# Moving the square root of the softmax shift in an attention backward kernel from ScalarE to a Newton step on VectorE, and spacing the stores of half of q

## The chip, the cores and the metric

One core of one Trainium2 chip. The metric is the device time in microseconds (us) of one execution. Kernels that are compared ran alternately on the same chip. Engine names in the profile: PE is TensorE, PEld its weight loads, DVE is VectorE, ACT is ScalarE, POOL is GpSimd, SP is SyncE, whose queue (SPq) carries transfers. The granted clock is the share of its full speed at which TensorE was allowed to run; "half clock" is 0.5 of it. The semaphore record is the trace's list of the times at which transfers report that they have landed. A pool is a region of on-chip memory from which the kernel takes its tiles.

## The reference

It is the forward pass and all gradients of two blocks on the same tokens: A, a linear attention, and B, a softmax attention with 16 heads of 28 columns that share one k and one v. Only B matters here.

```python
# S = 2048 tokens, D = 448, H = 16 heads, Dh = 28; all bf16
q = (x @ wq).reshape(B, S, H, Dh).transpose(0, 2, 1, 3)
k = x @ wk                              # one k and one v for all heads
v = x @ wv
scores = einsum("bhqd,bkd->bhqk", q, k) * Dh ** -0.5
p = softmax(scores)
o = einsum("bhqk,bkd->bhqd", p, v)
out_b = o.transpose(0, 2, 1, 3).reshape(B, S, H * Dh) @ wo
# ... and the vjp of concatenate([out_a, out_b]) for grad_out
```

The kernel computes exp(score - shift) with a shift for each query and head that is an upper bound of the scores, |q| times the largest |k|. The shift cancels when the row is normalised, so it need not be exact. That square root is what the change moves.

## The kernel before

Three parts follow one another: the linear attention (to about 200 us), a preparation (to 220 us) and the attention core of 512 steps (to 1003 us), with the last gradients behind it. The preparation computes q in four chunks of 512 tokens, writes the shift into spare rows of q, and brings q into token order in DRAM (qn_d), from where the core loads it back (qX).

```python
    def phase_B_pre(pa, cA, awk, psA, io):
        # ... k, v, and the largest |k|^2 per head in kmax2
        for qc in range(NQC):                                  # four chunks of 512 tokens
            # ... q of the chunk: matmuls, ACT copies to qT, DVE squares, row sums in pn
            shift = shifts[qc]
            nc.scalar.activation(out=shift, in_=pn[0:H, :], func=ACT.Sqrt, scale=kmax2[:, 0:1])      # L592
            for g in range(4):
                nc.gpsimd.dma_start(qT[:, g, qs].rearrange(...)[:, 0, :], shift[4 * g:4 * g + 4, :])  # L594
            if qc % 2:                                         # half of q: four transposes, one 1 MB store
                q2 = slice((qc - 1) * 512, (qc + 1) * 512)
                t2 = slice(4 * qc - 4, 4 * qc + 4)
                for g in range(4):
                    nc.sync.dma_start_transpose(qn[:, t2, g * P:(g + 1) * P], qT[:, g, q2])           # L599
                nc.sync.dma_start(qn_d[q2, :].rearrange("(t p) c -> p t c", p=P), qn[:, t2, :])       # L600
    # ... (cut)
    with ExitStack() as pa:                     # buffers of phase A and of the preparation, released together
        # psA ...
        cA = pa.enter_context(tc.tile_pool(name="cA", bufs=1, side="right"))    # holds xa and ga
        cB = pa.enter_context(tc.tile_pool(name="cB", bufs=1, side="right"))    # holds gaB, here the home of qn
        # ...
        phase_B_pre(pa, cA, awk, psA, io)
    # ... the core opens its own pools in the space that is now free: Exp's output eT, its transposes eN, ...
            tc.keep_in_program_order(nc.scalar.activation(out=ex[:], in_=ex[:], func=ACT.Exp))        # dummy Exp
            for u in range(NU + 28):
                # ... scores of step u on PE; a projection of grad_out rides along in some of the first 128 steps
                if hasS:
                    nc.scalar.activation(out=eT(u)[:, 0, :], in_=sp[0][:, :], func=ACT.Exp, scale=scale)   # L904
                # ... (the kernel goes on with the products of step u - 16)
                for a in {10: (0,), 14: (2,), 18: (1,), 22: (3,)}.get(u, ()) or {34: (0,), 42: (2,), 50: (1,), 58: (3,)}.get(u % 64, ()) * (u < 448):
                    # ... qX[qc] quarter a <- qn_d on POOL's queue                                       # L917
                if u == 70:
                    nc.gpsimd.dma_start(wo, ...)
                # ...
                if hasS:
                    # the second Exp of the step (L944), and every fourth step:
                    if u % 4 == 3:
                        nc.sync.dma_start_transpose(ENs[u // 4 % 6][:, :, :], ...)                       # L946
```

## Time and profile before

| | before |
|---|---|
| time, median of the runs beside the changed kernel | 1078.49 us (1077.77 to 1079.88, 4 runs) |
| profiled span, granted PE clock | 1079.1 us, 0.995 |
| first Exp of the core | 220.51 us |
| steps 16, 64, 384, 511 | 241.84, 323.72, 809.95, 1003.18 us |
| from step 511 to the end | 76.0 us |

A step time is the start of the first Exp activation of that step. The granted clock in the 40 slices of the page, in tenths, then the row of Exp in the page's list of the costliest groups (columns: times, mean ns of one, then idle time ahead of it and what ended most of it):

```profile
PEclk9999999998999999999999999999999999999999
...
L904 ACT ACTIVATE eT<-sps 128x512 bf16<-128x512 f32 x512 | 312.6, 611 | 22.9 <-PE dps L653 10.7
```

Exp of the whole core idles 22.9 us, ended most often by a matmul. Second, the reciprocals that this kernel has already, from the groups by form:

```profile
L795 DVE RECIPROCAL rl<-sps 128x4 f32<-128x4 f32 x64 | 10.1, 158 | 0.7 <-ACT eT L904 0.6
L320 DVE RECIPROCAL rden<-rden 128x64 f32<-128x64 f32 x4 | 2.2, 550 | 0.1
```

These two rows are 4 and 64 elements long on every partition. Third, a mark from POOL's timeline that lies before anything that the change touches; it lets one measure the preparation by itself, because the beginning of the program differs by up to 3.9 us between profiled executions (this mark comes at 190.96 in e1 and at 194.90 in e6):

```profile
192.82 0.54 POOL L522 DMA_DIRECT2D wkvT_d<-ga  x1
```

From this mark to the first Exp the kernel before takes 220.51 - 192.82 = 27.69 us.

### The profile page before, as it was taken

Reading aid. Unit: us, or ns where it says so; the run is one execution under the profiler, and the core shown is the slowest. Engines: PE = TensorE matmul, PEld = TensorE weight load, DVE = VectorE, ACT = ScalarE, POOL = GpSimd, SP = SyncE. Lnnn points to the kernel's source line nnn. Section 1 sums busy time; section 2 is a strip of 40 time slices with the busy share of each in tenths; the row PEclk is TensorE's granted clock in tenths of the full one; section 3 lists DMA queues with packets and bytes.
Section 4 is the critical chain, followed back from the end, with each engine's and each line's share of the span. In section 5 each row is a group of like instructions: output and inputs, shape, how many; then the busy total and the mean of one; then the engine's idle time right before and its main releaser. Section 6 shows DMA issues by size and latency. Waiting matters only on the chain.

```text
span 1079.1 us, 40135 instructions
## 1 busy us (share of the span) xinstructions
PE 1027.6 (95%) x16326; PEld 489.1 (45%) x16329; DVE 895.5 (83%) x1792; ACT 876.7 (81%) x1744; POOL 772.1 (72%) x1014
## 2 busy tenths in 40 slices
PE   9999999998999999999999999999999999999998
PEld 5555455443444444444444444444444444444434
DVE  7897400447999999999999999999999999999943
ACT  6463122577999999999999999999999999999622
POOL 6001243327888888888988888988998899888881
PEclk9999999998999999999999999999999999999999
DMA  9979899499999999999999999999999999999973
GB/s 239 165 131 195 161 196 193 88 215 169 202 210 198 179 190 187 197 188 201 183 187 191 201 188 194 204 184 182 193 203 186 193 194 193 196 177 180 221 140 92
DMA packets 669026, 199.36 MB, mean 185 GB/s; under 512 B 646008, under 2 KB 664736, under 8 KB 668840
## 3 DMA queue, kind: packets, MB, share of 16 engines
q1 hardware_dynamic: 656296, 175.23, 95.5%
q0 software_dynamic: 7584, 17.59, 6.9%
q10 hardware_dynamic: 4960, 3.96, 1.4%
q8 instruction: 128, 2.10, 0.8%
q14 instruction: 58, 0.48, 0.2%
HBM read 20.99 MB, written 12.94 MB: 31 GB/s over the span
## 4 chain that ended last, share of the span: by engine, by line
PE 34%; POOL 18%; ACT 18%; DVE 14%; issue 12%; DMA 4%; DVEq 0%; ACTq 0%; POOLq 0%; SPq 0%
POOL dsT L912 13%; PE agen L81 13%; ACT cp L911 9%; ACT eT L944 7%; DVE dsx L975 6%; PE sps L653 5%; PE aacc L81 4%; PE oq L653 4%; DVE dsT L909 3%; DMA eN<-eT 2%; PE dv_acc L653 2%; POOL prod L800 1%; PE dps L653 1%; DMA out_dram<-dsT 1%; DVE R L929 1%
## 5 line engine op out<-in xcount | busy, mean ns | idle before, releaser
L912 POOL TENSOR_TENSOR dsT<-cp,eT 128x512 bf16<-128x512 bf16 x512 | 588.4, 1157 | 104.5 <-ACT cp L911 98.6
L975 DVE STREAM_TRANSPOSE dsx<-dsT 128x512 f32<-128x512 f32 x512 | 357.7, 699 | 2.3 <-DVE R L723 0.2
L653 PEld LDWEIGHTS <-R 128*32 128x32 bf16 (+1 forms) x9184 | 229.5, 94 | 278.8 <-issue 238.7
L909 DVE TENSOR_TENSOR dsT<-dps,eT 128x512 bf16<-128x512 f32 x512 | 341.6, 667 | 16.5 <-PE dps L653 11.7
L904 ACT ACTIVATE eT<-sps 128x512 bf16<-128x512 f32 x512 | 312.6, 611 | 22.9 <-PE dps L653 10.7
L911 ACT ACTIVATE cp<-dps 128x512 bf16<-128x512 f32 x512 | 314.2, 614 | 12.0 <-PE dps L653 10.9
L944 ACT ACTIVATE eT<-sps 128x512 bf16<-128x512 f32 x512 | 320.3, 626 | 0.0
L653 PE MATMUL dk_acc<-dsx,qX 32*32 32x512 bf16 x4096 | 268.3, 376 | 0.0
L653 PE MATMUL dps<-doT,R 32*128 32x256 bf16 x2048 | 248.7, 270 | 1.9 <-ACT cp L911 0.8
L653 PE MATMUL sps<-R,R 32*128 32x256 bf16 (+1 forms) x2240 | 222.1, 274 | 7.6 <-DVE R L879 1.7
L653 PE MATMUL oq<-eT,R 128*32 128x256 bf16 x2048 | 158.3, 275 | 1.4 <-issue 1.4
L653 PE MATMUL oq<-dsT,R 128*32 128x256 bf16 x2048 | 157.1, 275 | 0.1
L653 PEld LDWEIGHTS <-qX 32*32 32x32 bf16 x4096 | 79.8, 89 | 114.4 <-issue 54.1
L653 PE MATMUL dv_acc<-eN,don 128*32 128x512 bf16 x1024 | 98.1, 381 | 3.8 <-DMA eN<-eT 3.8
L81 PEld LDWEIGHTS <-R 128*128 128x128 bf16 (+1 forms) x525 | 41.5, 98 | 41.7 <-issue 12.2
L406 POOL COPY pk<-R 128x256 bf16<-128x256 bf16 x4 | 1.6, 399 | 73.2 <-DVE R L366 73.1
L653 PEld LDWEIGHTS <-don 128*32 128x32 bf16 x1024 | 33.8, 97 | 5.0 <-issue 4.5
L422 DVE TENSOR_TENSOR osb<-aacc,pr 64x448 bf16<-64x448 f32 x2 | 1.2, 616 | 41.1 <-ACT pr L421 24.9
L800 POOL TENSOR_TENSOR prod<-R,oTs 128x128 f32<-128x128 bf16 x64 | 28.0, 438 | 7.7 <-DVE oTs L796 7.4
L929 DVE TENSOR_SCALAR R<-oq 64x256 bf16<-64x256 f32 x64 | 27.3, 427 | 3.6 <-PE oq L653 1.6
L817 PE MATMUL sps<-identB,don 128*32 128x128 bf16 x256 | 18.6, 224 | 12.3 <-POOL don L809 8.4
L81 PE MATMUL agen<-R,R 128*128 128x448 bf16 x128 | 28.6, 352 | 0.0
(232 smaller groups left out, 978.7 us busy)
## 6 DMA issues: line engine op xcount, KB each, us to landing
qX<-qn_d POOLq DMA_DIRECT2D x32, 256.0 KB, 4.3
out_dram<-osb ACTq DMA_DIRECT2D x22, 112.0 KB
qn_d<-gaT SPq DMA_DIRECT2D x2, 1024.0 KB
eN<-eT SPq DMA_TRANSPOSE x128
xa<-in_A_x_dram SPq DMA_DIRECT2D x8, 224.0 KB
ga<-in_grad_out_dram SPq DMA_DIRECT2D x4, 448.0 KB
xa<-in_grad_out_dram POOLq DMA_DIRECT2D x4, 448.0 KB, 12.2
out_dram<-wdq POOLq DMA_DIRECT2D x8, 224.0 KB, 6.3
```

What stands on the lines that cost most here:

```text
L81: nc.tensor.matmul(out_ap, lhsT=lhsT, rhs=rhs, start=start, stop=stop, tile_position=(0, 0))
L406: nc.gpsimd.tensor_copy(out=pk[:, t4, D:512], in_=gqn[:, t4, 3 * P:D])
L653: nc.tensor.matmul(out, lhsT=lhsT, rhs=rhs, start=start, stop=stop, tile_position=pos, skip_group_check=True)
L800: nc.gpsimd.tensor_tensor(out=prod[b][:], in0=dnv, in1=os_, op=ALU.mult)
L817: nc.tensor.transpose(tp2[q:q + 32, qb * P:(qb + 1) * P], don[b][:, qb, h, :], identB[:, :], tile_position=(0, q))
L904: nc.scalar.activation(out=eT(u)[:, 0, :], in_=sp[0][:, :], func=ACT.Exp, scale=scale)
L909: nc.vector.tensor_tensor(out=dst[:, 0, :], in0=dp[0][:, :], in1=ew[:, 0, :], op=ALU.mult)
L911: nc.scalar.activation(out=cp[:, :], in_=dp[1][:, :], func=ACT.Copy)
L912: nc.gpsimd.tensor_tensor(out=dst[:, 1, :], in0=cp[:, :], in1=ew[:, 1, :], op=ALU.mult)
L929: nc.vector.tensor_scalar(out=qT_B[g][64 * hp:64 * hp + 64, qc * 256:(qc + 1) * 256], in0=oq[64:128, 0:256], scalar1=scale, scalar2=None, ...
L944: nc.scalar.activation(out=eT(u)[:, 1, :], in_=sp[1][:, :], func=ACT.Exp, scale=scale)
L975: nc.vector.transpose(out=dsx[b][:, tp, :, :, :].rearrange("p h t c -> p (h t c)").bitcast(F32), in_=dsT[y][:, :, :].rearrange("p h c -> p ...
```

## The change

The intent: ACT loaded the table for Sqrt (at 204.10) and, at the core's entry, the one for Exp (1.28 us at 219.10), while PE waited. The change computes the root on DVE from the bit pattern (a shift gives a first value, one Newton step refines it), does the last of the four roots inside the core, and takes the second half of q off the entry: it is transposed into a buffer of the core and stored in four pieces of 256 KB, steps 34 to 58. It also lets the accumulators of the core rotate in the preparation's PSUM pool.

```diff
-        return xbT, wq_pad, rep, bsel, gaB, ga[:, 8:12, :]
+        return xbT, wq_pad, rep, bsel, xa[:, 0:8, :], ga[:, 8:12, :], [flat(gaB[:, 2 * i:2 * i + 2, :]).bitcast(F32) for i in range(3)]
...
-            shift = shifts[qc]
-            nc.scalar.activation(out=shift, in_=pn[0:H, :], func=ACT.Sqrt, scale=kmax2[:, 0:1])
-            # ... shift rows, and for both halves: four transposes, one store
+            if qc == NQC - 1:
+                break
+            q_shift(pn, shifts[qc], qs, tmp)
+            if qc == 1:
+                for g in range(4):
+                    nc.sync.dma_start_transpose(qn[:, :, g * P:(g + 1) * P], qT[:, g, 0:1024])
+                nc.sync.dma_start(qn_d[0:1024, :].rearrange("(t p) c -> p t c", p=P), qn)
...
+    def q_shift(pn, shift, qs, tmp):
+        a, y, r = (t[0:H, :] for t in tmp)
+        nc.scalar.activation(out=a, in_=pn[0:H, :], func=ACT.Identity, bias=eps[:, 0:1], scale=kmax2[:, 0:1])
+        nc.vector.tensor_scalar(out=y.bitcast(mybir.dt.int32), in0=a.bitcast(mybir.dt.int32), scalar1=1, scalar2=None,
+                                op0=ALU.logical_shift_right)
+        nc.vector.tensor_scalar(out=y, in0=y, scalar1=0.485 * 2.0 ** 63.5, scalar2=None, op0=ALU.mult)
+        nc.vector.reciprocal(out=r, in_=y)
+        nc.vector.tensor_tensor(out=r, in0=r, in1=a, op=ALU.mult)
+        nc.vector.scalar_tensor_tensor(out=shift, in0=r, scalar=0.25, in1=y, op0=ALU.mult, op1=ALU.add)
+        # ... the four small writes of the shift, as before
...
-        psA = psc.enter_context(tc.tile_pool(name="psAcc", bufs=1, space=bass.MemoryType.PSUM))
+        # psA of the preparation stays open; SB, DB, oq, dk_acc are taken from it, dv_acc at u == 1
...
-            tc.keep_in_program_order(nc.scalar.activation(out=ex[:], in_=ex[:], func=ACT.Exp))
+            qn = pqb_.tile([P, 8, 512], BF16, name="qX")
+            for g in range(4):
+                nc.sync.dma_start_transpose(qn[:, :, g * P:(g + 1) * P], R1[:, g, 1024:2048])
...
+                if u == 1:
+                    q_shift(*last_shift, [...])                # the last chunk, after the first Exp of step 1
+                    dv_acc = psA.tile([P, 512], F32, name="aacc")
...
+                for n in {34: (0,), 42: (1,), 50: (2,), 58: (3,)}.get(u, ()):
+                    nc.gpsimd.dma_start(qn_d[1024 + 256 * n:1280 + 256 * n, :].rearrange("(t p) c -> p t c", p=P),
+                                        qn[:, 2 * n:2 * n + 2, :])
-                for a in {10: (0,), 14: (2,), 18: (1,), 22: (3,)}.get(u, ()) or {34: (0,), ...}.get(u % 64, ()) * (u < 448):
+                for a in {10: (0,), 14: (2,), 18: (1,), 22: (3,), 66: (0,), 70: (2,), 74: (1,), 78: (3,)}.get(u, ()) or {
+                        34: (0,), 42: (2,), 50: (1,), 58: (3,)}.get(u % 64, ()) * (96 < u < 448):
-                if u == 70:
+                if u == 86:
```

## The prediction

> **What bounds the kernel now.** I read the page first, then the busy time by stretch, then the timeline of the stretch that the change touches, then the chain of waits and the matmul timeline there.
>
> ```profile
> PE 1027.6 (95%) x16326; PEld 489.1 (45%) x16329; DVE 895.5 (83%) x1792; ACT 876.7 (81%) x1744; POOL 772.1 (72%) x1014
> ...
> PE   9999999998999999999999999999999999999998
> DVE  7897400447999999999999999999999999999943
> ACT  6463122577999999999999999999999999999622
> ```
>
> From slice 10 on every engine is near full: that is the attention core, 512 steps u, each with two Exp activations of 128x512. In front of it lie the linear-attention part and a short preparation (slices 7 and 8). The change touches the preparation's end and the core's first 80 steps only. By stretch (columns: us, busy time of PE, PEld, DVE, ACT, POOL, then the granted clock, DMA share, GB/s):
>
> ```profile
> 218.00:226.00 8.00, 5.84 (x46) 2.56 (x45) 2.22 (x5) 6.17 (x11) 2.85 (x7) 0.79 0.87 203
> ...
> 250.00:270.00 20.00, 16.88 (x274) 7.29 (x275) 14.61 (x29) 14.57 (x29) 13.27 (x16) 0.84 1.20 185
> ...
> 400.00:1000.00 600.00, 576.23 (x11316) 267.20 (x11304) 584.90 (x1136) 593.07 (x1188) 529.75 (x630) 1.00 1.13 191
> ```
>
> In the steady core ACT is busy 593 of 600 us, so any start-up delay of ACT that is not made up moves the end one for one. Only the first and second rows show slack and a reduced clock. The entry itself:
>
> ```profile
> 212.47 5.94 SPq L599 DMA_TRANSPOSE gaT<-R  x4
> ...
> 218.41 0.68 ACT L592 ACTIVATE R<-aacc,kmax 16x512 bf16<-16x512 f32 x1 [0.93 <-PE aacc L81]
> ...
> 219.10 1.28 ACT L883 ACT_TABLE_LOAD   x1
> 219.28 0.49 PE L653 MATMUL sps<-R,R 32*128 32x256 bf16 x5 [0.79 <-DVE R L605]
> ...
> 220.51 0.58 ACT L904 ACTIVATE eT<-sps 128x512 bf16<-128x512 f32 x1
> ...
> 220.64 0.36 SPq L600 DMA_DIRECT2D qn_d<-gaT  x1
> 221.14 0.37 PE L653 MATMUL sps<-R,R 32*128 32x256 bf16 x3 [1.37 <-ACT eT L904]
> ```
>
> The last Sqrt (L592) ends at 219.09, the table for Exp is loaded, and the first Exp of the core starts at 220.51. It starts BEFORE the store of the first half of q (L600, issued 220.64): in this kernel Exp does not wait for that store. Remember this. Later in the entry the matmuls wait twice for transposes of Exp's output:
>
> ```profile
> 249.97 1.04 PE L653 MATMUL dv_acc<-eN,don 128*32 128x512 bf16 x6 [1.35 <-DMA eN<-eT]
> ...
> 265.91 0.61 PE L653 MATMUL dv_acc<-eN,don 128*32 128x512 bf16 x6 [2.41 <-DMA eN<-eT]
> ```
>
> They are late because one queue carries, one after the other, q's eight transposes, two 1 MB stores and then these. Counting the L904 activations gives the step times: u=0 at 220.51, u=16 at 241.84, u=64 at 323.72, u=128 at 422.89; the steady pace is about 1.52 us, and 1.545 where projections still ride along. So 48 steps from u=16 should take 74.2 us and take 81.9: 7.7 us are lost there.
>
> **What the skill says.** "ScalarE: Activation LUTs", section What ACT_TABLE_LOAD costs: about 1283 ns each, plus a drain; the trace has 1.28 us. Section Table sets: copy and identity stand in every set, so Identity needs no switch; the built program of after has one table load where before has three, which agrees. "TensorE: Matmul & The Clock Gate", section The HAM clock gate: after idling, the array runs at half clock for a window of about 3.4 us. The 0.79 above is one such window in 8 us: (8 - 3.41/2)/8 = 0.79; and 250 to 270 at 0.84 fits two. "DMA: Bandwidth & Descriptors", section Issuing engines are not separate DMA queues: moving stores to another issuing engine relieves no DMA engine, only the order. The DMA share, above 1.1 in the steady core, agrees.
>
> **The change part by part.**
> (1) Removed: the Sqrt, two table loads of 1.28 us and the dummy Exp (0.20). Only the second load lies at the entry: 218.41 to 220.51 could shrink to a start near 218.7, at most 1.8 us, and PE's idle 0.79 and 1.37 us would go with it, also because the score banks now rotate in the pool of the preparation.
> (2) Added: per chunk, one Identity (0.67 as Sqrt had) and five VectorE operations on 16x512 f32. By the rows for similar work (reduce of 16x512: 672 ns; reciprocal of 128x64: 550; f32 sum of 64x448: 616) I take 0.6 us each: 3 us a chunk, four times. VectorE has room (3.4 busy of 8 us from 210 to 218), so this is latency. But the built program of after puts the Identity of chunk 1 BEHIND the four q copies of chunk 2, and two squares of the next chunk between its five operations. Before, that activation starts at 209.82. After: the fourth copy ends about 212.9, Identity 213.6, the chain about 217.2. From 210.48 (end of the activation) to the first transpose at 212.47 took 2.0 us, so the transposes of the first half start near 219.3 instead of 212.5.
> (3) Moved: the first half of q in token order now lies in the first 8 KB of xa, not in gaT. xa's space is reused by Exp's output tiles. The wait list of the first Exp in the built after-program names the store of that half; in before its list ends at older transfers. So the first Exp must wait: transposes start 219.3, plus 8.15 (before: 212.47 to landing of the fourth at 220.62 by the semaphore record) = 227.4; store 5.2 (220.64 to 225.80 in the same record) = 232.6. First Exp at 232.5 instead of 220.5: **+12.0**. The gain of (1) is buried beneath it.
> (4) The first 16 steps took 21.3 us with one half-clock window. After a 12 us stop PE certainly starts cold, for one to two windows (each costs up to 1.7 us), and the last chunk's five VectorE operations (3 us) sit in front of the projection copies at u=1: **+1.9**.
> (5) The second 1 MB store leaves the queue in front of the second Exp transpose, and with Exp 12 us late the queue has drained. Both waits at u=20 and u=28 go: step 21 took 3.78 us and step 29 4.19, steps 30 and 31 2.25 and 1.83 at half clock, against 1.5 to 1.6: 2.2 + 2.6 + 0.7 = **-5.5**. A further stop of 1.4 us at u=49 (PE, "issue", while a q load is in flight) may or may not recur: **-0.5**.
> (6) Four stores of 256 KB on POOL's queue at u=34 to 58, four loads of q moved to u=66 to 78: about 4 x 0.6 us more on POOL and denser loads: **+0.5**.
> Sum: 1078.1 + 12.0 + 1.9 - 5.5 - 0.5 + 0.5 = 1086.5. I take 1085, as the first half's transposes and store are now less disturbed and may be quicker.
>
> **The rivals.**
> R1, the intent: Exp follows the last copies at once, no table load, no half clock, store out of the way. It would give -1.8, -1.7, -5.5: 1069 to 1071. For it: the listed waits are real and are the only visible DMA waits. Against it: the wait list in (3). It holds only if the store lands by 219, which needs transposes before about 206, when chunk 1 is not computed yet.
> R2, the wait exists but the store is not the bound: transposes unhindered take 6 us and the store 4: Exp at 229.5, +9; with all of (5) regained, 1081 to 1083.
> R3, the late start leads to a new queue behind it: q's second four transposes, the last shift's small writes (which wait for them on POOL) and q loads at u=10 to 22 now meet the Exp transposes; the waits at u=20 and 28 stay. Then nothing is regained: 1091 to 1093.
> R4, VectorE's chain delays the squares and PE in the preparation: at most 1 to 2 us, and hidden beneath the 12.
>
> **Range and chances.** 1082 (R2) to 1087 is the body; R3 is the upper tail, a partly right R1 the lower. 1078 to 1092 should hold it 8 times in 10. 2% is 21.6 us: faster would need under 1056.5, more than the whole loss of the entry (about 12); slower over 1099.6, twice my delay. So 0.01, 0.97, 0.02.
>
> **What would show it.** The timeline of ACT: first Exp near 232, its wait ended by the DMA qn_d<-xa; if it starts at 219, step (3) is wrong and R1 holds. SP's timeline: first transpose of q near 219, store near 227. The clock: a half-speed window right at the first Exp. PE's waits for eN<-eT: gone (5), or still there (R3). u=16 near 255.7, u=64 near 332. Two table loads less, none near the entry. The steady pace from 400 to 1000 must not move; if it does, the prediction is wrong in kind.

## The result

The changed kernel is correct and takes 1103.89 us (1101.12 to 1105.31, 4 runs) against 1078.49. The ratio is 1.0231, 95% interval 1.0207 to 1.0255: slower. A ratio is the mean time of one kernel's runs over that of the other's runs of the same rounds, so not quite the ratio of the medians. Executions over 1.5% slower than the fastest of the same kernel are left out of the means. The profiled run of the changed kernel is its fastest (1101.12), span 1099.4 us, clock 0.983, and that of the kernel before (1080.88) is slower than its four timed runs, so the profiles differ by 20.3 us where the medians differ by 25.4. For the other 5 us no trace was kept.

The page of the changed kernel, the rows that answer to those of before (busy time by engine, the clock by slice, the row of Exp), and then two groups by form:

```profile
PE 1032.9 (94%) x16329; PEld 490.5 (45%) x16329; DVE 915.8 (83%) x1812; ACT 874.9 (80%) x1741; POOL 773.8 (70%) x1018
...
PEclk9999999959899999999999999999999999999999
...
L913 ACT ACTIVATE eT<-aacc 128x512 bf16<-128x512 f32 x512 | 312.9, 611 | 44.5 <-DMA qn_d<-xa 14.8 <-PE aacc L660 11.3 <-PE agen L660 11.2
```

```profile
L612 DVE RECIPROCAL gaT<-gaT 16x512 f32<-16x512 f32 x3 | 10.0, 3335 | 0.0
L613 DVE TENSOR_TENSOR gaT<-gaT 16x512 f32<-16x512 f32 x3 | 2.0, 666 | 0.0
```

Exp's idle time has doubled from 22.9 to 44.5 us, and 14.8 us of it is one wait for a transfer. The clock has one slice at half speed (5 in the ninth slice). DVE has 20.3 us more work, of which four reciprocals are 13.3: each takes 3.33 us, not 0.6. The entry, from the timeline:

```profile
191.12 0.53 POOL L523 DMA_DIRECT2D wkvT_d<-ga  x1
...
219.97 3.33 DVE L612 RECIPROCAL gaT<-gaT 16x512 f32<-16x512 f32 x1
220.35 5.56 SPq L596 DMA_TRANSPOSE xa<-R  x4
...
227.85 0.36 SPq L597 DMA_DIRECT2D qn_d<-xa  x1
228.37 7.02 SPq L892 DMA_TRANSPOSE qX<-R  x4
232.78 0.60 ACT L913 ACTIVATE eT<-aacc 128x512 bf16<-128x512 f32 x1 [14.75 <-DMA qn_d<-xa]
233.43 0.58 PE L660 MATMUL aacc<-R,R 32*128 32x256 bf16 x3 [13.89 <-ACT eT L913]
...
236.09 3.34 DVE L612 RECIPROCAL dsT<-dsT 16x512 f32<-16x512 f32 x1
...
241.25 1.01 PE L82 MATMUL agen<-R,R 128*128 128x256 bf16 x4 [3.26 <-DVE R L886]
...
242.83 0.60 ACT L913 ACTIVATE eT<-aacc 128x512 bf16<-128x512 f32 x1 [3.73 <-PE aacc L660]
```

Read from the top: the mark comes at 191.12, so this execution is 1.70 us ahead of the one before when the preparation starts. The transposes of the first half start at 220.35 (before: 212.47), the store at 227.85, and the first Exp at 232.78, right behind the landing of that store, which the semaphore record of the trace puts at 232.22. From the mark to the first Exp it is 41.66 us against 27.69, so 13.97 more. PE stands still 13.89 us. Then, inside the core, the fourth reciprocal (236.09) keeps the projection copies (L886) from running, PE waits for them 3.26 us and Exp 3.73 us.

The busy time by stretch, same columns as in the prediction:

```profile
218.00:226.00 8.00, 1.02 (x3) 0.28 (x3) 7.12 (x10) 0.03 (x1) 3.09 (x8) 0.60 0.56 104
226.00:234.00 8.00, 0.57 (x4) 0.17 (x4) 0.00 (x0) 1.22 (x3) 1.93 (x4) 0.50 0.89 230
234.00:250.00 16.00, 12.74 (x77) 5.12 (x76) 8.16 (x12) 7.69 (x15) 2.81 (x5) 0.50 0.63 117
...
400.00:1000.00 600.00, 574.67 (x11280) 266.67 (x11269) 583.27 (x1131) 591.30 (x1184) 528.14 (x628) 1.00 1.14 191
```

The clock is at half from 219.57 to 250.29, by the clock records 30.7 us in one piece, also through the 16 us in which PE is again busy for 12.74. The steady stretch has the same pace as before, as predicted, up to a rise after step 384 that is told below.

Where the 20.3 us of the profiled spans come from, as the difference of the step times of the two kernels: +12.27 at step 0, +13.14 at step 3, +16.56 at step 4, +19.51 at step 8, +19.44 at step 16, +17.17 at step 21, +21.50 at step 28, +19.07 at step 32, +18.02 at step 50, +18.38 at step 64, +18.59 at step 384, +19.93 at step 448, +20.32 at step 511, and nothing after it (76.0 and 75.9 us from there to the end). The rise at step 28 is a wait of PE for a load of q, from the list of waits between 190 and 360 us:

```profile
PE agen L660 <- DMA qX<-qn_d: 3.0, 1, 3.0
```

And the small rise near step 446 starts with this POOL row, the 32nd and last load of q, which has no idle time ahead of it in the kernel before:

```profile
919.83 0.58 POOL L934 DMA_DIRECT2D qX<-qn_d  x1 [1.30 <-issue]
```

### The profile page after: what moved, and what is told of

It reads as the page before. It is cut to its first block, busy times and chain, and to the rows that moved or that the text cites. A ratio compares the mean times of both kernels' runs of the same rounds, so it can differ in the third digit from the quotient of the medians.

```text
span 1099.4 us, 40155 instructions
## 1 busy us (share of the span) xinstructions
PE 1032.9 (94%) x16329; PEld 490.5 (45%) x16329; DVE 915.8 (83%) x1812; ACT 874.9 (80%) x1741; POOL 773.8 (70%) x1018
## 4 chain that ended last, share of the span: by engine, by line
PE 36%; ACT 19%; POOL 17%; DVE 14%; issue 10%; DMA 2%; SPq 0%; ACTq 0%; DVEq 0%; POOLq 0%
PE agen L82 13%; POOL dsT L925 13%; ACT cp L924 9%; ACT eT L961 7%; PE aacc L660 7%; PE agen L660 7%; PE aacc L82 6%; DVE dsx L992 5%; DVE dsT L922 3%; ACT eT L913 1%; POOL prod L807 1%; POOL don L810 1%; PE aacc L824 1%; DVE R L946 1%; DVE oTs L943 1%
## 5 line engine op out<-in xcount | busy, mean ns | idle before, releaser
L922 DVE TENSOR_TENSOR dsT<-agen,eT 128x512 bf16<-128x512 f32 x512 | 341.4, 667 | 15.7 <-PE agen L660 10.8
L913 ACT ACTIVATE eT<-aacc 128x512 bf16<-128x512 f32 x512 | 312.9, 611 | 44.5 <-DMA qn_d<-xa 14.8
L924 ACT ACTIVATE cp<-agen 128x512 bf16<-128x512 f32 x512 | 315.1, 615 | 12.0 <-PE agen L660 11.0
L961 ACT ACTIVATE eT<-aacc 128x512 bf16<-128x512 f32 x512 | 321.5, 628 | 0.0
L660 PE MATMUL agen<-dsx,qX 32*32 32x512 bf16 x4096 | 269.6, 377 | 3.0 <-DMA qX<-qn_d 3.0
L660 PE MATMUL agen<-doT,R 32*128 32x256 bf16 x2048 | 249.1, 270 | 2.2 <-DVE dsT L922 1.1
L660 PE MATMUL aacc<-R,R 32*128 32x256 bf16 (+1 forms) x2240 | 223.3, 275 | 19.8 <-ACT eT L913 13.9
L660 PE MATMUL agen<-eT,R 128*32 128x256 bf16 x2048 | 158.9, 276 | 0.0
L660 PE MATMUL agen<-dsT,R 128*32 128x256 bf16 x2048 | 156.9, 275 | 0.1
L660 PE MATMUL aacc<-eN,don 128*32 128x512 bf16 x1024 | 97.5, 381 | 0.1
L82 PE MATMUL agen<-R,R 128*128 128x448 bf16 (+1 forms) x188 | 40.7, 348 | 3.7 <-DVE R L886 3.3
L946 DVE TENSOR_SCALAR R<-agen 64x256 bf16<-64x256 f32 x64 | 27.3, 427 | 3.6 <-PE agen L660 1.6
```

Of the source, the lines that this page charges most:

```text
L82: nc.tensor.matmul(out_ap, lhsT=lhsT, rhs=rhs, start=start, stop=stop, tile_position=(0, 0))
L660: nc.tensor.matmul(out, lhsT=lhsT, rhs=rhs, start=start, stop=stop, tile_position=pos, skip_group_check=True)
L922: nc.vector.tensor_tensor(out=dst[:, 0, :], in0=dp[0][:, :], in1=ew[:, 0, :], op=ALU.mult)
L924: nc.scalar.activation(out=cp[:, :], in_=dp[1][:, :], func=ACT.Copy)
L946: nc.vector.tensor_scalar(out=qT_B[g][64 * hp:64 * hp + 64, qc * 256:(qc + 1) * 256], in0=oq[64:128, 0:256], scalar1=scale, scalar2=None, ...
L961: nc.scalar.activation(out=eT(u)[:, 1, :], in_=sp[1][:, :], func=ACT.Exp, scale=scale)
```

## The experiments

Theory A: the loss is the sum of the release of the pool that holds q (first Exp late), of the reciprocals (3.33 us each, two of them ahead of the first transposes, one in the entry of the core), and of what follows from their stops. Its rivals are named in each expectation: the store itself and not the pool, the cold clock, or the spaced half and its transfers. Step differences below are to the profile of the kernel before that is shown above; each is one execution against one, from different rounds of runs. "From the mark" is the time from the write wkvT_d<-ga to the first Exp.

| kernel | time, median (range), us | ratio to before [95%] | span | first Exp | from the mark | step 16 | step 64 | step 511 |
|---|---|---|---|---|---|---|---|---|
| before | 1078.49 | 1 | 1079.1 | 220.51 | 27.69 | 0 | 0 | 0 |
| change | 1103.89 (1101.12 to 1105.31) | 1.0231 [1.0207, 1.0255] | 1099.4 | 232.78 | 41.66 | +19.44 | +18.38 | +20.32 |
| e1 store outside | 1102.90 (1097.90 to 1106.72) | 1.0194 [1.0154, 1.0235] | 1096.2 | 229.12 | 38.16 | +14.39 | +14.70 | +17.52 |
| e2 pool free | 1091.57 (1088.93 to 1098.20) | 1.0087 [1.0042, 1.0132] | 1089.9 | 219.48 | 28.51 | +8.90 | +6.02 | +11.77 |
| e3 no Newton | 1086.91 (1082.21 to 1094.50) | 1.0041 [0.9989, 1.0094] | 1085.8 | 227.46 | 34.24 | +7.28 | +3.62 | +7.29 |
| e4 filler | 1101.25 (1096.83 to 1105.55) | 1.0167 [1.0122, 1.0211] | 1095.1 | 232.60 | 41.55 | +19.27 | +12.50 | +15.33 |
| e5 both | 1078.21 (1076.28 to 1080.24) | 0.9965 [0.9927, 1.0004] | 1075.8 | 218.24 | 26.58 | -2.24 | -4.74 | -2.31 |
| e6 before, two-op shift | 1082.49 (1081.60 to 1086.50) | 1.0009 [0.9975, 1.0044] | 1080.4 | 224.25 | 29.35 | +3.84 | +1.72 | +1.77 |
| e7 before, spaced half | 1085.18 (1081.94 to 1087.38) | 1.0025 [0.9990, 1.0059] | 1083.0 | 221.23 | 27.73 | +1.98 | -1.22 | +4.02 |
| e8 e6 and e7 | 1086.07 (1081.57 to 1086.18) | 1.0025 [0.9990, 1.0060] | 1084.4 | 222.16 | 29.37 | +1.75 | +2.97 | +5.94 |
| e9 change, early loads | 1097.97 (1096.78 to 1101.62) | 1.0165 [1.0136, 1.0194] | 1096.0 | 235.06 | 41.62 | +20.34 | +13.74 | +17.16 |
| e10 e5, stores by SP | 1074.47 (1069.40 to 1085.50) | 0.9921 [0.9893, 0.9950] | 1068.9 | 219.95 | 26.58 | -1.72 | -9.69 | -9.12 |
| e11 e5, early loads | 1082.53 (1078.63 to 1082.98) | 0.9999 [0.9976, 1.0022] | 1080.6 | 219.82 | 26.59 | -1.86 | -2.84 | +2.06 |
| e12 e10 and e11 | 1074.83 (1071.32 to 1077.01) | 0.9935 [0.9911, 0.9959] | 1075.3 | 219.96 | 26.59 | -1.72 | -3.32 | -2.71 |

All twelve are correct. The kernel before ran beside e1 to e4 at a median of 1081.37 us, beside e5 to e8 at 1082.91 and beside e9 to e12 at 1081.64, each time on another chip, so ratios compare better than medians across the three groups. One of e10's six runs (1085.50) was slow and is not in its ratio.

### e1: the stored half out of the pool, its shift rows left in

```diff
-        return xbT, wq_pad, rep, bsel, xa[:, 0:8, :], ga[:, 8:12, :], [...]
+        return xbT, wq_pad, rep, bsel, gaB[:, 8:16, :], ga[:, 8:12, :], [...]
```

> Kernel after with one edit: the first half of q in token order lies in rows 8 to 16 of gaT (another pool) instead of in xa, so the wait list of the first Exp no longer names the 1 MB store, but it still names the small writes of chunk 2's shift. Theory A (the first Exp is held by everything still in flight in the pool whose space it takes, the store last): first Exp at 229.1 instead of 232.8 (those writes landed at 229.05 in after), time 1099 to 1101; q's second transposes now wait for the store instead (start about 232 instead of 228.4). Rival B (the store alone held it): first Exp at about 219.5, time near 1088. Rival C (Exp was held by something else, the store only came last by chance): first Exp stays at 232 to 233, 1104.

Measured: the first Exp at 229.12. The waits between 190 and 360 us say what it waits for now:

```profile
ACT eT L913 <- DMA R<-ga: 11.3, 1, 11.3
```

R<-ga are the four small writes of chunk 2's shift, out of ga, which lies in the same pool cA as xa. The semaphore record has the last of them at 228.90 (229.05 in the change). So it is not this store that Exp waits for, it is the release of the whole pool: whatever is still in flight out of cA. In the kernel before the same wait list names chunk 2's writes too:

```profile
214.84 2.24 POOL L594 DMA_DIRECT2D R<-ga  x4 [1.64 <-ACT ga L592]
```

They land at 218.00, 218.76, 219.60 and 220.14, and ACT's check of its waits ends at 220.39, in the same hundredth of a microsecond as the table load (219.10 to 220.39). So in the kernel before, too, the first Exp (220.51) starts as soon as the pool is released; behind the table load nobody saw it. The profile of this run is 3.2 us better than the change's, the ratio 0.004; the four timed runs (1097.90 to 1106.72) do not tell it from the change.

### e2: nothing of the preparation's end in the pool that Exp's buffers take over

```diff
-        return xbT, wq_pad, rep, bsel, xa[:, 0:8, :], ga[:, 8:12, :], [...]
+        return xbT, wq_pad, rep, bsel, gaB[:, 8:16, :], gaB[:, 6:8, :], [...]
-        shifts = [flat(sh)[0:H, i * 512:(i + 1) * 512] for i in range(NQC - 1)] + ...
+        shifts = [flat(sh)[0:H, i % 2 * 512:i % 2 * 512 + 512] for i in range(NQC - 1)] + ...
# and the two qX pools change places, so that the second half of q does not fall on gaB's bytes in use
```

> As e1, and the shifts of chunks 0 to 2 lie in gaT too, and the two pools for q's tiles change places, so that neither the store nor the shift's writes stand in the first Exp's wait list. The Newton step with its reciprocal (3.33 us each) stays, in the preparation and at u=1. Theory A: first Exp at 219 to 220 (when the matmuls of the last chunk and the first scores are done), no long half-clock stretch: 13 us from the entry and some 3 to 4 us from the clock; time 1085 to 1089. Rival D (the reciprocal in VectorE's queue is what costs, by way of squares and projection copies): the first Exp comes earlier but is given back, time over 1095.

Measured: the first Exp at 219.48, 13.3 us earlier than in the change, with no transfer in its way, although the transposes start as late as in the change (220.19). The gain at step 16 is 10.5 us, not 13.3, because the Newton step now shows at full length. The timeline of e2:

```profile
219.48 0.60 ACT L913 ACTIVATE eT<-aacc 128x512 bf16<-128x512 f32 x1 [1.61 <-PE aacc L82]
219.81 3.33 DVE L612 RECIPROCAL gaT<-gaT 16x512 f32<-16x512 f32 x1
...
225.59 3.34 DVE L612 RECIPROCAL dsT<-dsT 16x512 f32<-16x512 f32 x1
...
230.75 1.01 PE L82 MATMUL agen<-R,R 128*128 128x256 bf16 x4 [6.06 <-DVE R L886]
...
232.33 0.60 ACT L913 ACTIVATE eT<-aacc 128x512 bf16<-128x512 f32 x1 [6.52 <-PE aacc L660]
```

Two reciprocals and their followers lie between the first steps' projection copies: Exp stops for 6.52 us. Theory A holds for the pool, and the time, 1089.9 profiled, lies just above the expected range for this reason. What I expected of the clock was wrong: it stays at half from 219.22 to 239.70. Why cB, which is released at the same place, does not hold Exp is not shown.

### e3: the changed kernel without the Newton step

The first value from the bit pattern alone, within 3% of the root on either side, so no longer strictly an upper bound (the result was still correct): two DVE operations a chunk instead of five, no reciprocal.

```diff
-        nc.vector.tensor_scalar(out=y, in0=y, scalar1=0.485 * 2.0 ** 63.5, scalar2=None, op0=ALU.mult)
-        nc.vector.reciprocal(out=r, in_=y)
-        nc.vector.tensor_tensor(out=r, in0=r, in1=a, op=ALU.mult)
-        nc.vector.scalar_tensor_tensor(out=shift, in0=r, scalar=0.25, in1=y, op0=ALU.mult, op1=ALU.add)
+        nc.vector.tensor_scalar(out=shift, in0=y, scalar1=0.97 * 2.0 ** 63.5, scalar2=None, op0=ALU.mult)
```

> Kernel after without the Newton step: the shift is the scaled bit pattern alone (within 3% of the root, which is enough for a bound that the softmax takes out again); two VectorE operations of 0.41 us in place of five with a reciprocal of 3.33 us. The first half stays in xa. Theory A with the reciprocal as the mis-sized term: first transposes of q at about 215 instead of 220.35, store and first Exp 5.5 us earlier (near 227.3), the wait of 3.26 us of a projection at u=3 for VectorE gone: time about 1095. Rival (the reciprocal lies beside other work): first Exp and time unchanged within 1 us, 1103.

Measured: 1085.8 profiled, 13.6 us better than the change, far more than expected. It has two sources. In the preparation, the transposes start 20.75 us after the mark instead of 29.23, so 8.48 us earlier, and the first Exp 7.42 us earlier from the mark. In the core, the difference to before goes from +6.95 at step 0 to +7.28 at step 16, where the change went from +12.27 to +19.44: the 7.2 us of the first eight steps are gone too. The pool wait is still there, now 9.05 us and still for the store:

```profile
227.46 0.60 ACT L910 ACTIVATE eT<-aacc 128x512 bf16<-128x512 f32 x1 [9.05 <-DMA qn_d<-xa]
```

e2 and e3 take 9.5 and 13.6 us off the profiled span singly. Together that is 23.1; e5 below measures 23.6. The timed runs are less tidy: the ratio falls by 0.0144 in e2, by 0.0190 in e3 and by 0.0266 in e5, less than the sum.

### e4: keep PE warm through the stop

```diff
+                if u == 1:
+                    for _ in range(55):
+                        mm(dk_acc[:, :], R4[:, 0, 0:P], R4[:, 0, :])
                 rows_SD(u, sp, dp)
```

The results of these matmuls are overwritten. 

> Kernel after with 55 matmuls of 128x512 on a bank that is free at that time, issued at the head of u=1, while TensorE would wait for the first Exp (their result is overwritten, outputs stay right). First Exp stays at 232.8. Theory (the array went cold in the wait and stayed at half clock until 250.3, and this costs): no half-clock stretch between 233 and 250; the first 8 steps take about 14 us instead of 17.8 (10.6 in before, plus 3.3 for the reciprocal); time about 1100. Rival (the half clock costs nothing as other engines bind): steps and time unchanged, 1104.

Measured, busy time by stretch as above:

```profile
218.00:226.00 8.00, 8.00 (x39) 3.54 (x38) 7.05 (x10) 0.00 (x0) 3.18 (x8) 1.00 0.57 108
226.00:234.00 8.00, 5.01 (x25) 2.04 (x24) 0.00 (x0) 1.40 (x3) 1.87 (x4) 0.94 0.88 229
234.00:250.00 16.00, 12.74 (x78) 5.02 (x78) 8.17 (x12) 7.69 (x15) 2.83 (x5) 0.50 0.62 116
```

The filler ends at 230, and 3 us later the clock drops all the same, from 233.06 to 250.13. The steps 0 to 24 agree with the change within 0.2 us, so the half clock of the stop itself, 219 to 233, cost nothing. What the half clock after 233 costs this run cannot tell; e1, e7 and e9 can (see the part on the prediction). The 6 us that e4 is ahead at step 64 came later: at step 28 the wait for the q load is absent. The load was issued at 272.61, in the change at 272.80, and landed 4.2 us later instead of 8.9. The code of the two is the same there, so this is a difference between executions.

### e5: e2 and e3 together

> The changed kernel with the first half of q in the pool whose buffers the core does not take over, and with the shift from two VectorE operations (no reciprocal). Theory A (the loss of 20 us is the pool's release, the two-to-four reciprocals of 3.3 us in the entry, and the half clock that follows their stops; the two parts were +12 and +6 when taken away singly): first Exp at 217 to 219.5, no stop over 1 us in the steps 1 to 8, step 16 within 1 us of the kernel before, step 64 2 to 5 us ahead of it, and 1.3 us given back near step 446 as in all five kernels with the spaced stores; 1074 to 1078 us. Rival B (half clock and late q loads come from the second half's transposes inside the core, whatever the shift costs): step 16 still 4 us or more behind, 1083 to 1087 us.

Measured: theory A, on nearly every point. First Exp at 218.24; 2.24 us ahead of the kernel before from step 4 to step 16 (1.16 of it because this execution came to the mark earlier); clock at half for one window of 3.41 us only at the entry; 4.74 ahead at step 64; 2.1 us given back between steps 444 and 451, more than the 1.3 expected. 1075.8 profiled, ratio 0.9965 with an interval that touches 1. So up to step 384 the change's loss is the pool and the Newton step; what it loses after that (1.7 us) is still there (2.3 in e5).

### e6: the kernel before with the two-operation shift

```diff
-            nc.scalar.activation(out=shift, in_=pn[0:H, :], func=ACT.Sqrt, scale=kmax2[:, 0:1])
+            nc.scalar.activation(out=a, in_=pn[0:H, :], func=ACT.Identity, bias=eps[:, 0:1], scale=kmax2[:, 0:1])
+            nc.vector.tensor_scalar(..., op0=ALU.logical_shift_right)
+            nc.vector.tensor_scalar(out=shift, in0=y, scalar1=0.97 * 2.0 ** 63.5, scalar2=None, op0=ALU.mult)
...
-            tc.keep_in_program_order(nc.scalar.activation(out=ex[:], in_=ex[:], func=ACT.Exp))
```

> The kernel before, its Sqrt and its three table loads replaced by one Identity and two VectorE operations a chunk, all still in the preparation; both stores of q as before. It measures alone what the tables at the entry are worth. Theory A: first Exp at 219 to 219.9 (0.6 to 1.5 us earlier, the part of 1.28 us of table load that is not behind other work), the waits for transposes of Exp's output at steps 20 and 28 still there (1.4 and 2.4 us), 1076 to 1078 us against 1078.5. Rival B (the load was the only thing in the way): first Exp at 218.4, 1075 to 1076 us.

A miss. The first Exp comes at 224.25. Of the 3.74 us, 2.08 lie before the mark (194.90 against 192.82, a difference of the executions), but from the mark it is 29.35 against 27.69 too: 1.66 us worse without the table load. The wait of Exp there:

```profile
224.25 0.60 ACT L907 ACTIVATE eT<-sps 128x512 bf16<-128x512 f32 x1 [2.49 <-DMA gaT<-R]
```

The profile names the transposes; the wait list of the built program names chunk 2's shift writes out of pool cA, the last of which landed at 223.73, against 220.14 in the kernel before: 28.83 us from the mark against 27.32, so 1.51 later. That is nearly the whole 1.66. So taking the table away gains nothing here, because the release of the pool was a bound of equal length already in the kernel before, and with the root on DVE it comes later still. What the table load alone is worth this run cannot say; in e5, which has neither the load nor the pool's wait, it is 26.58 us from the mark, 1.1 less than before. e5 also has the accumulators in the preparation's PSUM pool; no run takes that part of the change back by itself, so its share of the 1.1 is open. The time is the same as before, 1.0009.

### e7: the kernel before with only the second half spaced

The stores and loads as in the change, the pools exchanged as in e2; Sqrt and both halves' order otherwise as before.

> The kernel before, with only the second half of q changed as in the change: transposed inside the core, stored in four pieces at steps 34 to 58, its loads at steps 66 to 78. Sqrt stays. It measures alone what the spacing is worth. Theory A: the second store no longer lies in front of the transposes of Exp's output, so the waits at steps 20 and 28 go (2.2 and 2.6 us longer steps before): step 32 is 3 to 6 us ahead of the kernel before, about 1 to 1.5 us are given back near step 446, 1073 to 1076 us. Rival B (the transfers only change places and the q loads of steps 10 to 22 come late, as in the changed kernel): a stop at step 28 for qX<-qn_d, step 32 within 1.5 us of the kernel before, 1077 to 1080 us.

Measured: rival B. The wait for the transposed Exp output at step 20 goes, 2.3 us are regained at step 21, and at step 28 they are lost to a wait for the q load, which is 8.0 us under way (255.31 to 263.32). Step 32 is 0.53 ahead. Then the end: at the last load of q the same POOL stop of 1.30 us, and 4.6 us lost between steps 444 and 452, a half-clock window at 913 among them. The time is not distinguishable from before (1.0025), and not the 1073 to 1076 that I expected of it. This run also happens to have half clock from 223.66 to 230.49, without a Newton step, and loses 1.5 us in steps 4 and 5; that is used below.

### e8: e6 and e7 together

> The two parts together, each as in e6 and e7: the candidate for a version that beats both kernels. If they add up: first Exp at 219 to 219.9, step 32 4 to 7 us ahead of the kernel before, 1072 to 1075 us (ratio 0.994 to 0.997). If the entry's DMA traffic decides and not the order of the parts: no better than the better of the two parts, 1076 to 1078 us.

A miss, for the reasons of both: first Exp at 222.16 (29.37 from the mark, as e6), then a q load 12.3 us under way and 6.5 us of wait at step 28, and 2.8 us lost near step 446. 1.0025, no better than its parts.

### e9: the change, first loads of q earlier

```diff
-                for a in {10: (0,), 14: (2,), 18: (1,), 22: (3,), 66: ...
+                for a in {8: (0,), 11: (2,), 14: (1,), 18: (3,), 66: ...
```

> The changed kernel, with the four loads of q's first quarter issued at steps 8, 11, 14 and 18 instead of 10, 14, 18 and 22. Theory A (the stop at step 28, 4.4 us against the kernel before, is the last of these loads, 8.9 us under way and issued 9 us before it is needed): the wait for qX<-qn_d at step 28 goes, steps 28 to 31 run in 1.4 to 1.6 us each, the difference to the kernel before at step 32 falls from +19.1 to +13 to +15, profiled span 1093 to 1096 against 1099.4. Rival B (the transfers as a whole are short of room between steps 8 and 28): the stop only moves, to a wait for eN<-eT at step 20 or 28, and the difference stays above +17.5. The first 8 steps must not change in either.

Measured: the wait at step 28 is gone, and after the first Exp neither PE nor ACT waits for a transfer up to 360 us. From step 26 to step 32 the difference falls by 3.66 us (18.06 to 14.40), where it rose by 1.93 in the change. The span, 1096.0, is at the edge of what theory A gave; the preparation began 2.3 us later in this execution. The half clock lasted 27.3 us (221.56 to 248.87; 30.7 in the change), so it does not need the late load.

### e10: e5 with the four spaced stores on the other queue

```diff
-                    nc.gpsimd.dma_start(qn_d[1024 + 256 * n:1280 + 256 * n, :]...
+                    nc.sync.dma_start(qn_d[1024 + 256 * n:1280 + 256 * n, :]...
```

> As the kernel with free pool and no Newton step, but the four stores of q's second half issued by the queue of the Exp transposes instead of the POOL queue. All six kernels with four more POOL transfers stop 1.30 us at the same one of them, the 32nd load of q at step 442, and lose 1.3 to 5.4 us between steps 446 and 452; the two kernels without them do not. Theory A (a count of transfers on the POOL queue is reached earlier): the stop goes from step 442, the steps 446 to 452 run as before, and step 511 is as far ahead as step 384, about 4.5 us; 1072.5 to 1075 us. Rival B (the stop belongs to that load or to what it writes): it stays, 1.3 us or more lost there. In both, the transposes of Exp's output behind the four stores land 1 to 3 us later, which no wait should show.

Theory A holds in what it says of the stop. POOL's row of the last load of q, which had 1.30 or 1.31 us of idle time ahead of it in every kernel with the four extra POOL transfers:

```profile
890.60 0.58 POOL L931 DMA_DIRECT2D qX<-qn_d  x1
```

From step 384 to step 511 only 0.3 us are lost, where the ten kernels with the stores on POOL's queue, the change among them, lost 1.7 to 5.6. No transposed Exp output is waited for. It also had no wait at step 28, with the code up to step 34 the same as in e5: its last load of q took 5.0 us, that of e5 7.4. So 3.6 us of its lead (at step 32: 7.68 against 4.04) over e5 are the execution and not the edit; the timed runs spread accordingly. Ratio 0.9921, interval 0.9893 to 0.9950: with e12 (0.9935, overlapping intervals) the best of the kernels here, and it beats both, by less than 2%. One word of theory A is not borne out, the count: with the four stores on POOL's queue the stop is at its 99th transfer, but in this run, in e12 and in the two kernels without spaced stores the 99th transfer of that queue has no idle time ahead of it either. So the four stores bring the stop, and not by their number alone.

### e11: e5 with the early loads

> As the kernel with free pool and no Newton step (1075.8 profiled), with the four first loads of q at steps 8, 11, 14, 18. There the stop at step 28 was 2.8 us longer than in the kernel before. Theory A: the stop goes, step 32 is 7 to 9 us ahead of the kernel before instead of 4.0; profiled span 1071 to 1073. Rival B: the stop turns into one for eN<-eT, lead at step 32 below 5 us, 1075 to 1077.

Rival B. The list of waits:

```profile
PE aacc L657 <- DMA eN<-eT: 4.0, 1, 4.0
```

With the core starting 15 us earlier than in e9, three loads issued between 233.4 and 235.9 meet the second transpose of Exp's output: it takes 15.8 us (235.06 to 250.89) and PE waits at step 20. What helps the late kernel hurts the early one. 0.9999, and 1080.6 profiled, above rival B's 1075 to 1077.

### e12: e10 and e11 together

> Early loads and the stores by the other queue together, the candidate that should beat both kernels. If both theories A hold and add: first Exp near 218, step 32 7 to 9 us ahead, nothing lost at step 446, 1069.5 to 1072 us, ratio to the kernel before 0.991 to 0.994. If one fails: 1072 to 1075.

The stop near step 446 is gone as in e10, the wait at step 20 is there as in e11 (5.4 us). 1075.3 profiled, 0.9935: not better than e10. "If one fails" was right.

## Why the prediction was wrong

It said 1085 us, 1078 to 1092; the result is 1103.89. The working summed to +8.4 us; the profiled spans differ by +20.3. Step by step, with the term as predicted and as measured:

| step | predicted | measured |
|---|---|---|
| (3) first Exp later, step 0 | +12.0 | +12.27 |
| (4) first 16 steps | +1.9 | +7.17 (19.44 - 12.27) |
| (5) waits regained, steps 16 to 50 | -5.5 and -0.5 | -1.42 (18.02 - 19.44) |
| (6) denser transfers, rest of the core | +0.5 | +2.30 (20.32 - 18.02) |

**Step (3), the wait of the first Exp, was right** in place (232.5 against 232.78) and in what it waits for; that its size came out was partly luck. From the mark the first Exp is 13.97 us later, not 12.0. Two parts inside it were off and cancelled. From the mark the first transposes start 9.58 us later than before, where I had 6.8, and 8.48 of it are the Newton step's longer operations (e3); but this execution came to the mark 1.70 us early. And the transposes and the store were quicker than before (7.48 and 4.37 us instead of 8.15 and 5.16), as R2 had it, so R2's mechanism was there and too small. One sentence in it was wrong: I wrote that xa's space is reused by Exp's output tiles. By the addresses of the built program none of the five overlaps xa; e1 shows that the wait is for the release of the pool, with the store moved elsewhere and Exp waiting for another transfer out of the same pool.

**Step (2) is where it failed, and through it (4).** I took 0.6 us for each of the five DVE operations, and for the reciprocal I read it off a row of 128x64. That row has 64 elements on each partition, the new one 512; how many partitions there are does not count (6.5 ns an element below, with 128 partitions and with 16). From the two rows of the kernel before, (550 - 158) / (64 - 4) = 6.5 ns an element, so 158 + 508 x 6.5, about 3.5 us; measured 3.34. The number was in the profile. The Trainium skill offers a reason in "VectorE: DVE Perf Modes", section First, the fixed hardware budget: reciprocal is an iterative divide with a repeat count of 8. The measured 6.5 ns an element (3335 for 512) against 1.3 for the multiply of the same shape (666 ns for 512) agrees in kind with that, a factor of five; no run here shows the mechanism. The other four operations took 0.41 to 0.68 us, as assumed.

From that one number follows most of what the core's entry loses. In (4) I had "the last chunk's five VectorE operations (3 us)" hidden in 1.9. The fourth reciprocal lies before the projection copies, PE waits 3.26 us, and step 4 comes 3.42 us later than its predecessor would have it. Of the rest of the 7.2 us, 0.7 come at step 2 (e10 has nearly as much there at full clock) and 2.95 in steps 4 to 7, which are run at half clock. Without the reciprocal (e3) the clock is back 4.7 us after the first Exp and none of this is lost; with it the half clock lasts 17.5 us into the core (13.8 to 20.2 in the five kernels with the Newton step), where (4) had one or two windows of 3.4.

e4 failed to lift the clock there, but other traces tell the clock from the copies that still catch up. e7 has no Newton step and half clock in steps 4 and 5: it loses 1.06 and 0.46 us in them, the change 1.07 and 0.53. And e1 and e9, the same program as the change in these steps, have the clock back just before step 6 (at 242.89 and 248.87): their steps 6 and 7 take 2.38 us together, 2.47 in the kernel before, and 3.81 in the change, where the clock comes back at 250.29. So these 2.95 us belong to the half clock and not to the copies.

**Step (5) was right about what goes and wrong about what comes.** The wait at step 20 went (2.3 us), and the one for eN at step 28. But in its place came a wait for the last load of q of the first quarter, 3.0 us for PE and 4.4 at step 28. That is rival R3, which I had put in the upper tail with a different victim. e9 shows that an earlier issue removes it, e7 that it comes without any late start, e4 and e10 that it depends on whether that load takes 4 to 5 or 7 to 9 us. Half clock follows it (281.01 to 287.84); its share of the loss is not separated.

**Step (6)** missed the POOL stop at the last load. e10 and e12 against e5 and e11 show that it goes with the four stores when they leave POOL's queue. Why they bring it is not shown here; it is not their number alone (e10).

**The range.** The rivals were each an alternative to the sum; none let (3), (4) and R3 all go to the bad side. The chance of 0.02 for slower by over 2% rested on "twice my delay", which the reciprocal alone, 13.6 us by e3, nearly supplied. The part about the intent, R1, and step (1) overlooked that the table load was not alone in the way: the pool's release ended with it at 220.39, so the 1.8 us were not to be had from the table (e6 gained none). With both out of the way e5 gains 1.1 us from the mark, and e10 ends below the kernel before.

One reading in the prediction shows nothing: a DMA share above 1.1 is a mean over the engines, whoever issued the transfers, and does not bear on what moving them to another issuer does. e5 and e10 do: with the four stores on POOL's queue or on SP's the share is 1.18 and 1.16 from 270 to 320 us, about the same.

## What to carry to other kernels

Scale an operation's cost by the elements on one partition, and from two rows of the profile, before putting it in front of work that others wait for. When a buffer of a preparation moves, look up which pool it is in and what the next user of that pool's space waits for: the whole pool is released at once, and a transfer that seemed harmless becomes the bound as soon as it is late. Transfers that are taken out of one place should be followed to the queue in which they end up, up to the last step.

## What the Trainium skill lacked or had wrong

- "VectorE: DVE Perf Modes", section The perf-mode tier table: reciprocal is not in it. Measured, f32: 158 ns for 4 elements on a partition, 550 for 64, 3335 for 512, against 666 for a multiply of two 512-element inputs. The page's repeat count of 8 tells that it is slow, not how slow.
- "TensorE: Matmul & The Clock Gate", section What's actually happening: the clock is said to come back after one or more busy windows of about 3.4 us. Here it stayed at half for 30.7 us, through 16 us in which PE was busy 12.74 (busy time counted at half clock), and with the filler it fell again 3 us after the filler's end and stayed for 17.1 us. How busy a window must be to count as busy is not said.
- "DMA: Bandwidth & Descriptors", section Queues, rings and completion order: nothing on POOL stopping after a number of its own transfers. Here the last load of q, the 99th transfer on its queue, had 1.30 or 1.31 us of idle time ahead of it in all ten kernels with four more of them in the core; in the four without (before, e6, e10, e12) neither this load, the 95th there, nor their 99th transfer had any.
- The same page has no figure for how much the time of one such load varies beside other transfers: the same quarter of q, issued at the same step, was under way 4.2, 5.0, 7.4 and 8.9 us in four executions.
- No page says that a pool's release makes the next user wait for transfers still in flight out of it. The waits are part of the program as built, not of the chip; e1 and e2 show them, 9.6 us apart in the first Exp.
